# No-ops between row scatters, spins in narrower pieces, and a reordered start in a sorted-attention and expert-layer kernel

## The chip, the core and the metric

The kernel runs on one core of one Trainium2 chip. A core has a matrix engine (TensorE, PE in the profile), a vector engine (VectorE, DVE), a scalar engine (ScalarE, ACT), a general engine (GpSimd, POOL), an engine that mostly starts transfers (SyncE, SP) and 16 DMA engines. Each engine works through its own list of instructions in order and waits on semaphores for the others. The metric is the device time of one execution in microseconds; lower is better.

## What is computed

Two layers follow each other. The first is an attention whose key and value blocks are mixed by a matrix `P`, made from `sort_net` in five rounds of normalising; the second sends each of 3072 rows to one of 8 experts.

```python
# attention: batch 4, heads 8, sequence 768 in 8 blocks of 96, head size 64
for _ in range(5):
    P = exp(P - max(P, -1));  P = P / sum(P, -1);  P = P / sum(P, -2)
k_sorted = einsum('bhij,bhjcd->bhicd', P, k_b)        # the same for v
scores = q_b @ k_sb.T / sqrt(64)                      # within a block
x = softmax(scores) @ v_sb                            # -> 3072 rows of 512

# expert layer
logits = x @ w_gate + modality_bias[modality_id]
e_idx = argmax(logits);  gate_w = softmax(logits)[e_idx]
out[row] = gate_w * (relu(x @ w1[e_idx]) @ w2[e_idx]) # w1: 512x1024, w2: 1024x512
```

## The kernel before

The kernel is one straight program. Its parts, in the order of time:

1. Loads of q, k, v and of two experts' weights, issued by GpSimd; the five rounds on `P` on VectorE and ScalarE. Meanwhile TensorE multiplies ones ("spins"):

```python
wsrc = bass.AP(tensor=ones_bf.tensor, ..., ap=[ones_bf.ap[0], [0, 4], [1, 128]])   # 512 columns
def spin(n, after=None):
    for z in range(n):
        ins = nc.tensor.matmul(warm[:, z % 2], ones_bf, wsrc, start=True, stop=True)
        ...
spin(13)
for u in range(2):
    tq_pe(u)                       # transposes of q
spin(5)
...                                # in round 4: spin(4, e_ins)
```

2. The sort of k and v for the first half of the batch (`g0`: 10 jobs for k, then those for v), as matmuls into PSUM and copies out of it (L353 in the profile, matmuls L366 for k and L375 for v). `copy_out` lets a small balance decide between ScalarE and VectorE.

```python
for f, g, x0, kd in g0[:10]:       # k sort
    f(g, x0, kd)
scores(0); expo(0); mod_T()
load_k(1, 0); load_k(1, 1)
home_map(); spread_q(0, 1, nc.gpsimd); gate_w()
for n, (f, g, x0, kd) in enumerate(g0[10:]):   # v sort
    f(g, x0, kd)
    if n == 3:
        scores(1); expo(1)
```

3. 32 steps of attention. Step `u` does `scores(u)` (matmuls L418), `expo(u)` (ScalarE, L424) and `av(u - 1)` (matmuls L437, then VectorE L444 and L445). From step 16 on a step also runs one piece of the expert layer. Further work is hung onto steps: `at1` before `av`, `at2` after it. Four groups `m` of 8 steps each end in `gate_T`, `gate_L` (logits of the 768 rows of the group, four times 128 columns `c`), `choose(m)` (the best expert, on VectorE), `place(m)` and `table(m)`.

```python
for u in range(2, 32):
    p1, p2 = pace(u)               # (0, 0) before 16, then (1, 0)
    scores(u); expo(u)
    run_pieces(p1)
    for f, a in A1.get(u, []): f(*a)
    av(u - 1); prep_q(u + 2); prep_s(u + 3)
    run_pieces(p2)
    for f, a in A2.get(u, []): f(*a)
```

4. `place(m)` ranks the rows of a group within their experts (matmuls L502 to L509, VectorE L512 to L520) and sends them to a scratch buffer in DRAM, 96 rows to a scatter:

```python
def one(t):
    if t:
        if m:
            nc.gpsimd.memset(kT[0][:, 0:896], 0.0)   # L531; kT[0] is not read any more
        nc.gpsimd.nop()
    ins = nc.gpsimd.indirect_dma_start(out=xs_dram, ..., in_=xt.bitcast(I32)[:, t], ...)  # L533
for t in range(8):
    one(t)
```

`table(m)` (VectorE, L580 to L605, each on a few numbers) turns the counts into the start rows of the next expert pieces ("slots" of 256 rows); SyncE reads them and fetches the rows, transposed (L656). Slots 0 and 1 depend on group 0, slots 2 and 3 on group 1, 4 to 7 on group 2, 8 to 12 on group 3.

5. The expert layer: for each slot four pieces `mL1` (matmuls L689, relu on ScalarE L683 or VectorE L681) and two pieces `mL2` (matmuls L712, scaling L699 or L701, a scatter into the output L703). After `table(3)` every engine reads the number of rows left over and branches (L993); with this input there is none.

Of the kernel before, what the change touches and what calls it, by code (L numbers as in the profile page):

```python
# [17 lines left out]
def kernel(  # L18
# [13 lines left out]
    nc = tc.nc  # L32
# [41 lines left out]
    kT = [singles.tile([128, GC], BF16, tag=f"kT{g}", name=f"kT{g}") for g in range(2)]  # L74
# [6 lines left out]
    xTg = [singles.tile([128, 8, BLK], BF16, tag=f"xTg{z}", name=f"xTg{z}") for z in range(2)]  # L81
# [9 lines left out]
    def q_in(g, hh):  # L91
# [11 lines left out]
                                            ap=[[2 * BLK, NTL], [1, 2 * BLK]]))  # L103
# [44 lines left out]
    ones_bf = singles.tile([128, 128], BF16)  # L148
# [93 lines left out]
        eng(qT, tq.pop(u).rearrange("p t (i r) -> p i t r", r=16))  # L242

    warm = opsum.tile([128, 2, 512], FP32, tag="op", name="warm")
    wsrc = bass.AP(tensor=ones_bf.tensor, offset=ones_bf.offset, ap=[ones_bf.ap[0], [0, 4], [1, 128]])

    def spin(n, after=None):
        for z in range(n):
            ins = nc.tensor.matmul(warm[:, z % 2], ones_bf, wsrc, start=True, stop=True)
            if after is not None and z == 0:  # L250
                tc.add_manual_dep(ins.ins, after.ins.name, SYNC, reason="in step with the iterations")

    spin(13)
    for u in range(2):
        tq_pe(u)
    spin(5)
    for it in range(5):
        if it == 0:
            nc.vector.tensor_reduce(red, P_t, AX.X, ALU.max)
            nc.vector.tensor_tensor(P_t, P_t, red.broadcast_to([BH, NB, NB]), ALU.subtract)  # L260
        e_ins = nc.scalar.activation(P_t, P_t, ACT.Exp)
        if it == 4:
            spin(4, e_ins)
        if it == 3:
            tq_out(0, nc.scalar.copy)
        if it == 4:
            tq_out(1, nc.scalar.copy)
        for f in gap[it]:
            f()
        nc.vector.tensor_reduce(red, P_t, AX.X, ALU.add)  # L270
        nc.vector.reciprocal(red, red)
        nc.vector.tensor_tensor(P_t, P_t, red.broadcast_to([BH, NB, NB]), ALU.mult)
        nc.vector.tensor_reduce(red, P_swap, AX.X, ALU.add)
        nc.vector.reciprocal(red, red)
        colb = bass.AP(tensor=red.tensor, offset=red.offset,
                       ap=[red.ap[0], [0, NB], red.ap[1]])
        nc.vector.tensor_tensor(P_bf if it == 4 else P_t, P_t, colb, ALU.mult)
# [38 lines left out]
    def mod_T():  # L316
        tp = mipsum.tile([128, 64], BF16, tag="mi", name="modT")
        nc.tensor.transpose(tp[0:BLK, 0:NTL], modB.rearrange("b t r -> b (t r)"), ident[0:NTL, 0:NTL])
        nc.scalar.copy(modF, tp[0:BLK, 0:NTL])
# [20 lines left out]
    def use(act=0.0, dve=0.0):  # L340
        busy[0] += act
        busy[1] += dve
# [9 lines left out]
    def copy_out(dst, src, act, dve):  # L352
        (nc.scalar.copy if pick(act, dve) else nc.vector.tensor_copy)(dst, src)  # L353
# [54 lines left out]
    def scores(u):  # L408
        g, hf, h = unit(u)
        sc = scpsum.tile([128, 2, 512], FP32, tag="sc", name=f"sc{u}")  # L410
        qT = qTb[g][:, h * 768:(h + 1) * 768].rearrange("p (i f) -> p i f", i=NB)
        for j in range(4):
            i = hf * 4 + j
            x0 = (h * 8 + i) * BLK
            m = 128 if h * 8 + i < 63 else BLK
            for par in range(2):
                rows = slice(par * 64, (par + 1) * 64)
                nc.tensor.matmul(sc[0:m, par, j * BLK:(j + 1) * BLK],  # L418
                                 kT[g][rows, x0:x0 + m], qT[rows, i],
                                 start=True, stop=True)  # L420
        sc_tiles[u] = sc

    def expo(u):
        mark[0] = nc.scalar.activation(attnT[u % 2][:, 0:8 * BLK].rearrange("p (r f) -> p r f", r=2),  # L424
                             sc_tiles.pop(u)[0:BLK, :, 0:4 * BLK], ACT.Exp, scale=scale)
        use(act=0.82)
# [24 lines left out]
    def gate_T(m, c):  # L451
        tp = mipsum.tile([128, 8, BLK], BF16, tag="mi", name=f"gt{m}_{c}")
        for t in range(8):
            nc.tensor.transpose(tp[:, t], xb[m % 2][:, t, c * 128:(c + 1) * 128], ident[:BLK, :BLK])  # L454
        copy_out(xTg[c % 2], tp, 0.8, 0.56)

    def gate_L(m, c):
        lg = mipsum.tile([BLK, 8, E], FP32, tag="mi", name=f"lg{m}_{c}")
# [36 lines left out]
    def place(m):  # L495
        oh, ls = oh_t[m]
        xt = xb[m % 2]
        prev = ohs[m % 2]
        rk = mipsum.tile([128, 8, E], FP32, tag="mi", name=f"rk{m}")
        rkf = rk.rearrange("p t e -> p (t e)")  # L500
        pb = bass.AP(tensor=prev.tensor, offset=prev.offset, ap=[prev.ap[0], [0, 8], prev.ap[1]])
        nc.tensor.matmul(rkf, maskUT[0:BLK, :], oh.rearrange("p t e -> p (t e)"), start=True, stop=False,  # L502
                         skip_group_check=True)
        nc.tensor.matmul(rkf, ones_bf[0:BLK, :], ebase.rearrange("p t e -> p (t e)"), start=False, stop=False,
                         skip_group_check=True)
        nc.tensor.matmul(rk, ones_bf[0:BLK, :], pb, start=False, stop=False, skip_group_check=True)
        for t in range(7):
            ob = bass.AP(tensor=oh.tensor, offset=oh[:, t].offset, ap=[oh.ap[0], [0, 7 - t], [1, E]])
            nc.tensor.matmul(rk[:, t + 1:8], ones_bf[0:BLK, :], ob, start=False, stop=(t == 6),  # L509
                             skip_group_check=True)  # L510
        sel_r = small.tile([BLK, 8, E], FP32, tag="selr", name=f"selr{m}")
        nc.vector.tensor_tensor(sel_r, rk[0:BLK], oh, ALU.mult)  # L512
        dest = small.tile([BLK, 8], I32, tag="dest", name=f"dest{m}")
        dstf = small.tile([BLK, 8], FP32, tag="dstf", name=f"dstf{m}")
        nc.vector.tensor_reduce(dstf, sel_r, AX.X, ALU.add)
        nc.vector.tensor_copy(dest, dstf)
        sm = small.tile([BLK, 8, 1], FP32, tag="sm", name=f"sm{m}")
        nc.vector.tensor_reduce(sm, ls, AX.X, ALU.add)
        gcol = xt.bitcast(FP32)[:, :, Dm // 2 + 1:Dm // 2 + 2]
        nc.vector.reciprocal(gcol, sm)  # L520
        g, hf = m // 2, m % 2
        icol = xt.bitcast(I32)[:, :, Dm // 2]
        idm = idI.rearrange("p (b f j) -> p b f j", b=4, f=2)[:, 2 * g:2 * g + 2, hf]
        nc.gpsimd.tensor_copy(icol.rearrange("p (r j) -> p r j", r=2), idm)
        scat[m] = []
        use(dve=1.5)

        def one(t):
            if t:
                if m:  # L530
                    nc.gpsimd.memset(kT[0][:, 0:896], 0.0)  # L531
                nc.gpsimd.nop()
            ins = nc.gpsimd.indirect_dma_start(  # L533
                out=xs_dram, out_offset=bass.IndirectOffsetOnAxis(ap=dest[:, t:t + 1], axis=0),
                in_=xt.bitcast(I32)[:, t], in_offset=None)
            after = []
            tc.declare_no_dep(ins.ins, group="xs", reason="rows are disjoint", **({"keep": after} if after else {}))
            tc.add_to_no_dep_group("xs", ins.ins)
            for pre in after:
                tc.add_manual_dep(ins.ins, pre.name, SYNC, reason="rows leave at an even pace")  # L540
            scat[m].append(ins.ins)
        ones_[m] = one
        for t in range(8):
            one(t)
        nxt = ohs[(m + 1) % 2]
        ohsum = small.tile([BLK, E], FP32, tag="ohsum", name=f"ohsum{m}")
        nc.vector.tensor_reduce(ohsum, oh.rearrange("p t e -> p e t"), AX.X, ALU.add)
        nc.vector.tensor_tensor(nxt, ohsum, prev, ALU.add)
# [222 lines left out]
    g0 = jobs(0, kinds)  # L771
    for f, g, x0, kd in g0[:10]:
        f(g, x0, kd)
    scores(0)
    expo(0)
    mod_T()
    load_k(1, 0)
    load_k(1, 1)
    home_map()
# [2 lines left out]
    use(dve=-busy[1], act=-busy[0])  # L782
    for n, (f, g, x0, kd) in enumerate(g0[10:]):
        f(g, x0, kd)
        if n == 3:
            scores(1)
            expo(1)
    load_v(1)
# [37 lines left out]
    def at1(u, f, *a):  # L826
        A1.setdefault(u, []).append((f, a))

    def at2(u, f, *a):
        A2.setdefault(u, []).append((f, a))  # L830
# [8 lines left out]
    for m in range(4):  # L839
        for c in range(4):  # L840
            u = 8 * m + 2 * c + 3
# [10 lines left out]
    at2(8, *jb[1])  # L852
    at2(8, gate_T, 0, 3)
    at2(8, *jb[2])
    at2(8, gate_L, 0, 3)
    at2(8, choose, 0)
    at2(8, *jb[3])
    at1(9, place, 0)
    at2(3, make_bd, 1)
    at2(4, late_consts)  # L860
    j_at = [9] * 4 + [10] * 4 + [11] * 4 + [12] * 3 + [13] * 3 + [14] * 3 + [15] * 3
    for u, j in zip(j_at, jb[4:]):
        at2(u, *j)
    at2(17, place, 1)
    at1(26, place, 2)
    for m in range(3):
        at2(8 * m + 11, table_x, m)
# [161 lines left out]
```

## Time and profile before

| | |
|---|---|
| Timed, median of 3 | 200.13 us (199.83 to 202.01) |
| Profiled execution | 213.3 us |
| Mean granted TensorE clock in the profile | 0.899 |
| Row scatters L533 | 32, 931 ns each |
| Memsets L531 | 21, 862 ns each, 18.1 us in all |
| Expert matmuls L689 / L712 | 384 at 281 ns / 181 recorded at 391 and 382 ns |
| Spin matmuls L249 | 22 of 512 columns, 8.7 us |
| DMA queue of the loads and scatters | 23.10 MB, 48.5% of 16 engines' span |

The profile is one execution, and it is longer than the timed ones; it is read for the place and the cause of a wait. A busy time of PE is that of pipelined matmuls; PEld is the weight load, which goes beside them. `[2.34 <-issue]` behind an instruction says that its engine was idle for 2.34 us before it and what ended that; "issue" is time in which it waited for nothing that the profile shows. In a table of stretches each engine has its busy time and, in brackets, its instructions.

### The profile page before, as it was taken

Reading aid. Unit: us, or ns where it says so; the run is one execution under the profiler, and the core shown is the slowest. Engines: PE = TensorE matmul, PEld = TensorE weight load, DVE = VectorE, ACT = ScalarE, POOL = GpSimd, SP = SyncE. Lnnn points to the kernel's source line nnn. Section 1 sums busy time; section 2 is a strip of 40 time slices with the busy share of each in tenths; the row PEclk is TensorE's granted clock in tenths of the full one; section 3 lists DMA queues with packets and bytes.
Section 4 is the critical chain, followed back from the end, with each engine's and each line's share of the span. In section 5 each row is a group of like instructions: output and inputs, shape, how many; then the busy total and the mean of one; then the engine's idle time right before and its main releaser. Section 6 shows DMA issues by size and latency. Waiting matters only on the chain. (4 is left out here: it accounts for less than half of the span.)

```text
span 213.3 us, 5194 instructions
## 1 busy us (share of the span) xinstructions
PE 170.9 (80%) x2050; PEld 122.5 (57%) x2061; DVE 108.0 (51%) x331; ACT 93.7 (44%) x150; POOL 102.0 (48%) x139
## 2 busy tenths in 40 slices
PE   6476698777449987969599599999699999999910
PEld 2235597566329976738466475676566676765400
DVE  5977577746118787787277532557124222322200
ACT  2037468757108874946447332453213242223300
POOL 7901579901740040799408983279870623223230
PEclk9979799997855899999879658999999999999995
DMA  5999999999980559812532215853162993121210
GB/s 60 210 222 202 202 218 223 201 215 213 208 214 9 99 80 195 159 42 59 161 58 86 58 38 153 166 121 122 49 182 92 187 225 110 52 98 49 98 49 0
DMA packets 30160, 27.66 MB, mean 130 GB/s; under 512 B 18831, under 2 KB 25775, under 8 KB 29872
## 3 DMA queue, kind: packets, MB, share of 16 engines
q0 software_dynamic: 11792, 23.10, 48.5%
q1 hardware_dynamic: 18336, 4.16, 11.8%
q8 instruction: 17, 0.28, 0.5%
q14 instruction: 15, 0.12, 0.2%
HBM read 27.35 MB, written 10.52 MB: 178 GB/s over the span
## 5 line engine op out<-in xcount | busy, mean ns | idle before, releaser
L689 PE MATMUL hp<-xT,w 128*128 128x256 bf16 x384 | 49.0, 281 | 2.1 <-PEq L993 2.1
L703 POOL DMA_INDIRECT out_dram<-kvb,idg x25 | 24.6, 983 | 44.9 <-DVE kvb L701 21.2
L533 POOL DMA_INDIRECT xs_scratch<-xb,dest x32 | 29.8, 931 | 31.1 <-issue 29.1
L689 PEld LDWEIGHTS <-w 128*128 128x128 bf16 x384 | 37.2, 100 | 11.0 <-issue 2.3
L424 ACT ACTIVATE attnT<-sc 96x768 bf16<-96x768 f32 x32 | 26.0, 811 | 10.3 <-PE sc L418 10.1
L712 PE MATMUL yp<-w,hT 128*128 128x512 bf16 x90 | 23.0, 391 | 0.5 <-issue 0.2
L445 DVE TENSOR_TENSOR xb<-op,rs 96x512 bf16<-96x512 f32 x32 | 22.0, 687 | 1.3
L712 PE MATMUL yp<-w,qT 128*128 128x512 bf16 x91 | 22.3, 382 | 0.3 <-issue 0.2
L699 ACT ACTIVATE kvb<-yp,idg 128x512 f32<-128x512 f32 x15 | 10.3, 687 | 20.3 <-PE yp L712 19.0
L531 POOL MEMSET kT<- 128x896 bf16 x21 | 18.1, 862 | 0.0
L454 PE MATMUL gt<-ident,xb 96*128 96x96 bf16 x128 | 9.8, 225 | 10.1 <-DVE xb L445 9.7
L683 ACT ACTIVATE hT<-hp 128x512 bf16<-128x512 f32 x17 | 10.1, 595 | 15.1 <-PE hp L689 10.4
L681 DVE TENSOR_SCALAR qT<-hp 128x512 bf16<-128x512 f32 x10 | 6.9, 692 | 17.8 <-PE hp L689 17.8
L366 PE MATMUL ka<-bd,kvb 128*64 128x64 bf16 x384 | 10.4, 206 | 6.9 <-issue 5.6
L437 PE MATMUL op<-v_sb,attnT 96*128 96x65 bf16 x256 | 14.9, 206 | 1.3 <-DVE xb L445 0.9
L353 ACT CAST kT<-ka 128x512 bf16<-128x512 f32 (+1 forms) x16 | 9.3, 651 | 13.5 <-PE sc L418 8.1
L418 PE MATMUL sc<-qT,kT 64*128 64x96 bf16 (+1 forms) x256 | 12.9, 221 | 2.8 <-issue 1.8
L712 PEld LDWEIGHTS <-hT 128*128 128x128 bf16 x96 | 9.4, 101 | 9.9 <-issue 1.4
L701 DVE TENSOR_SCALAR kvb<-yp,idg 128x512 f32<-128x512 f32 x9 | 6.8, 751 | 16.3 <-PE yp L712 12.5
L683 ACT ACTIVATE qT<-hp 128x512 bf16<-128x512 f32 x14 | 8.2, 595 | 15.0 <-PE hp L689 11.1
L454 PEld LDWEIGHTS <-xb 96*128 96x128 bf16 x128 | 7.1, 107 | 13.4 <-DVE xb L445 12.1
L712 PEld LDWEIGHTS <-qT 128*128 128x128 bf16 x96 | 9.2, 99 | 9.6 <-issue 0.5
(182 smaller groups left out, 267.9 us busy)
## 6 DMA issues: line engine op xcount, KB each, us to landing
w<-in_moe_w_dram POOLq DMA_DIRECT2D x4, 1024.0 KB
kvb<-in_k_dram POOLq DMA_DIRECT2D x4, 768.0 KB
kvb<-in_v_dram POOLq DMA_DIRECT2D x2, 1536.0 KB
q_in<-in_q_dram POOLq DMA_DIRECT2D x4, 384.0 KB
xs_scratch<-zpad SPq DMA_DIRECT2D x3, 258.0 KB
v_sb<-in_q_dram POOLq DMA_DIRECT2D x4, 192.0 KB
v_sb<-in_q_dram POOLq DMA_DIRECT2D x2, 384.0 KB
xs_scratch<-xb,dest POOLq DMA_INDIRECT x32
```

Of the source, the lines that this page charges most:

```text
L366: nc.tensor.matmul(acc[par * 64:(par + 1) * 64, z], k_raw[:, (c0 + z) * D:(c0 + z + 1) * D], bd[g][:, par * 64:(par + 1) * 64], start=True ...
L418: nc.tensor.matmul(sc[0:m, par, j * BLK:(j + 1) * BLK], kT[g][rows, x0:x0 + m], qT[rows, i], start=True, stop=True)
L424: mark[0] = nc.scalar.activation(attnT[u % 2][:, 0:8 * BLK].rearrange("p (r f) -> p r f", r=2), sc_tiles.pop(u)[0:BLK, :, 0:4 * BLK], ACT. ...
L437: nc.tensor.matmul(ov[:, par, j], attnT[u % 2][:, c0:c0 + 128], v_sb[g][0:BLK, par * 64 + h * 8 + i, 0:D + 1], start=True, stop=True)
L445: nc.vector.tensor_tensor(xt[:, :, h * D:(h + 1) * D].rearrange("p (r j) d -> p r j d", r=2), ov[0:BLK, :, :, 0:D], rs.broadcast_to([BLK, ...
L454: nc.tensor.transpose(tp[:, t], xb[m % 2][:, t, c * 128:(c + 1) * 128], ident[:BLK, :BLK])
L531: nc.gpsimd.memset(kT[0][:, 0:896], 0.0)
L533: ins = nc.gpsimd.indirect_dma_start(out=xs_dram, out_offset=bass.IndirectOffsetOnAxis(ap=dest[:, t:t + 1], axis=0), in_=xt.bitcast(I32)[: ...
L683: mark[0] = nc.scalar.activation(dst, src, ACT.Relu)
L689: nc.tensor.matmul(hp[:, f], w_at(s, c * F + (2 * j + f) * 128, 128), xT_b[s % NX][:, c], start=(c == 0), stop=(c == 3))
L703: ins = nc.gpsimd.indirect_dma_start(out=out, out_offset=bass.IndirectOffsetOnAxis(ap=idg[:, t, 0:1], axis=0), in_=y, in_offset=None, boun ...
L712: nc.tensor.matmul(yp, hT_b[s % 2][:, fc, t * 128:(t + 1) * 128], w_at(s, 4 * F + fc * Dm, Dm), start=(fc == 0), stop=(fc == 7))
```

## The change

It has four parts.

- Between the later row scatters (groups 1 to 3) the memset of a strip that nobody reads is replaced by 11 no-ops of GpSimd. Both keep scatters apart; a no-op uses no memory.
- The spins multiply 128 columns at a time instead of 512, four times as often.
- At the start, two v-sort jobs stand ahead of the first scores, so that TensorE has work while the last copies of sorted k are made; the second scores move three jobs back.
- The chain from the last gate of group 0 to its ranking is rearranged: the last transposed copy of a group always goes to VectorE, and three more jobs of the second sort stand between its steps. `place(1)` moves from the end of step 17 to the first half of step 18.

```diff
-    wsrc = bass.AP(tensor=ones_bf.tensor, offset=ones_bf.offset, ap=[ones_bf.ap[0], [0, 4], [1, 128]])
-            ins = nc.tensor.matmul(warm[:, z % 2], ones_bf, wsrc, start=True, stop=True)
+            ins = nc.tensor.matmul(warm[:, z % 2, 0:128], ones_bf, ones_bf, start=True, stop=True)
-    spin(13)
+    spin(52)
...
-    spin(5)
+    spin(20)
...
-            spin(4, e_ins)
+            spin(16, e_ins)
... gate_T
-        copy_out(xTg[c % 2], tp, 0.8, 0.56)
+        if c == 3:
+            nc.vector.tensor_copy(xTg[c % 2], tp)
+            use(dve=0.56)
+        else:
+            copy_out(xTg[c % 2], tp, 0.8, 0.56)
... place
                 if m:
-                    nc.gpsimd.memset(kT[0][:, 0:896], 0.0)
+                    for _ in range(11):
+                        nc.gpsimd.nop(nofuse=True)
                 nc.gpsimd.nop()
... the start
-    scores(0)
-    expo(0)
-    mod_T()
     load_k(1, 0)
...
     for n, (f, g, x0, kd) in enumerate(g0[10:]):
         f(g, x0, kd)
-        if n == 3:
+        if n == 1:
+            scores(0)
+            expo(0)
+            mod_T()
+        if n == 6:
             scores(1)
             expo(1)
... steps 8 and 9
     at2(8, *jb[2])
+    at2(8, *jb[3])
     at2(8, gate_L, 0, 3)
     at2(8, choose, 0)
-    at2(8, *jb[3])
+    at2(8, *jb[4])
+    at1(9, lambda f, *a: f(*a), *jb[5])
+    at1(9, lambda f, *a: f(*a), *jb[6])
     at1(9, place, 0)
...
-    j_at = [9] * 4 + [10] * 4 + [11] * 4 + [12] * 3 + [13] * 3 + [14] * 3 + [15] * 3
-    for u, j in zip(j_at, jb[4:]):
+    j_at = [9] * 1 + [10] * 4 + [11] * 4 + [12] * 3 + [13] * 3 + [14] * 3 + [15] * 3
+    for u, j in zip(j_at, jb[7:]):
         at2(u, *j)
-    at2(17, place, 1)
+    at1(18, place, 1)
```

## The prediction, made before the changed kernel was run

> **What bounds the kernel now.** I read the page's busy shares first, then the stretches of 3 us, then the timeline around each stretch in which TensorE (PE) had little to do, and last the chain that ended last. The profiled execution took 213.3 us and the timed ones 200.13, so I use the profile for where time is lost and scale the total afterwards.
>
> ```profile
> PE 170.9 (80%) x2050; PEld 122.5 (57%) x2061; DVE 108.0 (51%) x331; ACT 93.7 (44%) x150; POOL 102.0 (48%) x139
> ```
>
> PE is busy 80% of the span, no other engine much over half. From 151.87 us on the chain of waits is a row of PE pieces (L689, L712) without holes, so the end is simply the end of PE's work: a hole or a cold stretch of PE before that point is paid in full, and one that is removed is gained, unless a transfer then comes last.
>
> The stretches show the holes (columns: stretch, length, PE, PEld, DVE, ACT and POOL busy with counts, granted PE clock, DMA share, GB/s):
>
> ```profile
> 93.00:96.00 3.00, 0.87 (x17) 0.55 (x16) 2.22 (x7) 0.78 (x2) 2.83 (x4) 1.00 0.11 33
> 102.00:105.00 3.00, 0.67 (x18) 0.47 (x16) 1.11 (x3) 0.20 (x1) 1.82 (x2) 1.00 0.49 140
> 117.00:120.00 3.00, 0.52 (x7) 0.52 (x8) 2.26 (x9) 0.67 (x2) 2.83 (x4) 0.87 0.12 33
> 120.00:123.00 3.00, 3.00 (x31) 2.32 (x30) 0.89 (x2) 1.61 (x2) 2.66 (x4) 0.50 0.26 71
> 123.00:126.00 3.00, 3.00 (x33) 2.36 (x31) 1.11 (x3) 1.40 (x2) 2.83 (x4) 0.50 0.12 34
> 126.00:129.00 3.00, 2.78 (x22) 1.81 (x22) 1.36 (x3) 0.60 (x1) 2.32 (x3) 0.50 0.23 66
> ```
>
> In two of the holes POOL is 94% busy and DVE long busy with few instructions; after the one at 117 the clock is at half for 9 us. The timeline says what DVE did (start, length, instruction, idle before and releaser):
>
> ```profile
> 115.33 1.36 DVE L581 TENSOR_SCALAR tb_ti<-tb_ti 1x8 int32<-1x8 int32 x1
> 115.81 0.86 POOL L531 MEMSET kT<- 128x896 bf16 x1
> 116.84 0.92 POOL L533 DMA_INDIRECT xs_scratch<-xb,dest  x1 [0.17 <-issue]
> 117.47 1.17 DVE L587 TENSOR_SCALAR tabR<-tb_r 1x4 int32<-1x4 f32 x1
> 117.75 0.86 POOL L531 MEMSET kT<- 128x896 bf16 x1
> 119.48 0.61 PEld L454 LDWEIGHTS <-xb 96*128 96x128 bf16 x8 [2.80 <-DVE xb L445]
> ```
>
> An operation on eight numbers takes 1.36 us and ends at 116.69; the memset ends at 116.67. The next ends at 118.64, the memset at 118.61. The same operation undisturbed takes 0.16 us. Both began while the scatter before the memset ran, so the scatter holds them up too, and the memset follows it with no gap. PE waits for the DVE work queued behind.
>
> The third place, and two smaller ones:
>
> ```profile
> 151.87 3.65 PE L689 MATMUL hp<-xT,w 128*128 128x256 bf16 x32 [2.09 <-PEq L993]
> 83.56 0.20 PE L502 MATMUL rk<-oh,maskUT 96*128 96x64 bf16 x1 [1.25 <-DVE oh L486]
> 22.20 0.25 PE L366 MATMUL ka<-bd,kvb 128*64 128x64 bf16 x4 [2.34 <-issue]
> ```
>
> The first is the branch on the count of left-over rows, which DVE computes at the end of table 3, among memsets. The second is ranking 1, asked for before its DVE chain is done. The third is PE without an instruction in the middle of a tile.
>
> **What the Trainium skill says.** (1) "Advanced Engine Details and Errata", section VectorE Performance Modes: the second Vector SBUF port is shared with GpSimd, and GpSimd instructions and two-port Vector instructions block each other. The trace agrees: the stretched DVE operations go from SBUF to SBUF, while L681, which reads PSUM, keeps its 0.69 us beside a memset at 97.84. (2) The same page, Sequencer and Instruction Queues: the sequencer queues engine instructions and executes control instructions itself meanwhile. The trace shows no no-ops, so it does not say whether they run beside a scatter. (3) "TensorE: Matmul & The Clock Gate", Part 1: after an idle window of about 3.4 us the clock falls to half. Here idle times of 2.3 and 2.5 us (at 102.2 and 117.0) were each followed by a drop, one of 2.1 us (at 93.3) was not, so it also depends on where the window lies. (4) "Runtime: NRT & Kernel Launch", Instruction fetch mechanics: instructions come in blocks of 256 (16 KiB). The instruction queue shows one packet of 16 KB at 20.01 us, inside the hole of 2.34 us.
>
> **The change, part by part.**
>
> *No-ops for memsets.* 21 memsets of 0.86 us go, seven each in placings 1 to 3, and 11 no-ops take each one's place. Small sequencer steps on SyncE (semaphore waits at 68.61, 68.68, 68.75, 68.82) follow each other at 70 ns, so I estimate 11 x 0.07 = 0.77 us. If they come after the scatter, the period is 0.92 + 0.30 (as in placing 0, which has no memset and a period of 1.22) + 0.77 = 1.99 us, against 1.95 now; if they run beside it, 1.22. So rows leave at about the same pace, or 7 x 0.73 = 5.1 us sooner per placing. What matters is DVE. A held operation can then start when the scatter ends instead of 0.86 us later.
> - Table 1: three held-up groups (L127, a pair of copies, 2.01 instead of 0.61 us; L582, 1.47; L587, 1.33), 3 x 0.86 = 2.6 us, more than the PE hole of 2.13. I leave 0.5 for scatters that still hold DVE: gain 1.6.
> - Table 2: L581 and L587, 2 x 0.86 = 1.7 of a hole of 2.52: gain 1.6.
> - Table 3: L582 (1.57) and L587 (1.32), 1.7 of a hole of 2.09: gain 1.5.
> - The clock after table 2: 9 us at 0.50 with PE 8.8 us busy, so 4.4 us lost. With a hole of 0.9 us I give even chances that it does not drop: 2.2.
> Sum 6.9.
>
> *Ranking 1 later by a piece.* Placing 1 moves behind the scores and one expert piece of step 18 (0.34 + 1.05 us). That fills most of the 1.25: gain 0.8. Its scatters start a little later; slot 2, which reads them, asks for its rows at 103.17 and first uses them at 113.97, so that is free.
>
> *Spins in pieces of 128.* 22 matmuls of 512 columns become 88 of 128: the same columns. At half clock 512 columns took 0.43 us, and six of 128 columns (L236, at 10.36) 0.82 us from the first start to the last end, about 0.11 each behind the first, four of which make 0.43. No time of its own, but 2 x 66 = 132 more PE instructions in front of everything, so that all block borders shift by half a block. That can shorten the hole at 19.86 or move it.
>
> *v sort ahead of the first scores.* At 22.45 PE is idle 0.84 us until the last copy of kT. Two v-sort tiles now go in there: up to 0.9.
>
> *First ranking.* gate_T(0,3) is copied on DVE (0.56) instead of ACT (0.80, behind two kT copies), and more sort jobs stand between its steps. PE holes of 0.39, 0.51 and 0.99 us from 45.75 to 49.7 are what can be filled.
>
> These last three lie before 63 us, where the DMA share stays near or above 1 (1.13, 1.27, 1.25 at 48, 51 and 57). The first expert rows travel behind the first expert's weights, and one scatter waited 1.78 us for them until 62.31. So front gains mostly end in a longer wait for rows: I count 0.3 of some 3.
>
> Total: 6.9 + 0.8 + 0.3 = 8.0 us in the profiled execution. The timed runs are 13 us shorter, so some of these holes must be smaller there, and a shorter hole can be taken over by the next wait. I take about 0.64 of it: 5.1 us, so **195.0 us**.
>
> **Rivals.**
> 1. *The scatter is what holds DVE.* All held operations began during a scatter. If no-ops run beside scatters, 0.92 of each 1.22 us is taken and DVE has only the gaps of 0.3 us. Then about a third of the 4.7 us of the three tables and little of the clock comes: 197 to 199. Against it: each held operation ended with the memset, not the scatter.
> 2. *Slow no-ops.* At 0.2 us each, the period is 3.4 us and the last rows leave 7 x 1.5 = 10 us later. Slot 8 has its rows asked for at 155.99 and used at 167.51, a reserve of about 8 us after some 4 of travel; PE that is 5 us ahead would wait: 202 to 205. Nothing on SyncE looks that slow.
> 3. *Fetching takes it back.* The shifted borders put a hole as at 19.86 into a place that counts, or the 231 no-ops make POOL wait for instructions during scatters: 1 to 3 us, 196 to 198.
> 4. *The cold stretch always goes* and the fetch hole too: 190 to 192.
>
> **Range and chances.** Case 4 sets the low end, 190.5; rivals 1 and 3 together nearly nothing gained, 200.0. The line for over 2% is 196.1, a little above my number; rivals 1 and 3 lie in the band, only rival 2 lies above it. Faster by over 2% 0.60, within 2% 0.33, slower 0.07.
>
> **What would show it.** Right: L581, L582 and L587 of every table below about 0.6 us; PE holes at tables 1 to 3 under 1 us; no half clock after table 2; scatters 1.2 or 2.0 us apart. The front steps: kT's last copy followed by v-sort matmuls, ranking 0 without a wait of 1 us, but the first L689 of slot 0 waiting for rows. Wrong: DVE operations that still end with a scatter after a microsecond; a scatter period over 2.5 us; or PE holes that return in the same sum at other lines, L454 or L689 behind a transfer above all.

## The result and the profile after

The changed kernel takes **192.98 us** (median of 4, 192.78 to 194.41), the kernel before 201.07 in the same comparison (199.83 to 203.62): a ratio of **0.9633** with a 95% interval of 0.9542 to 0.9724. The profiled execution took 191.1 us with a mean granted clock of 0.946. That of before was 22.2 us longer, much more than the timed difference of 8.1, so again the profiles say where and the times say how much.

The line of the page on TensorE (PE) and the others, after:

```profile
PE 160.8 (84%) x2127; PEld 122.1 (64%) x2127; DVE 100.6 (53%) x332; ACT 93.4 (49%) x149; POOL 83.3 (44%) x118
```

POOL has 21 instructions and 18.7 us less, of which the 21 memsets make 18.1. There is nothing in their place: the lists of GpSimd's instructions in the two built programs differ by these memsets alone, no no-op is in either or in the records of the traces (what took them out is not shown), and the scatters of groups 1 to 3 now follow each other 1.21 us apart, as those of group 0 always did.

Stretches of 3 us of the changed kernel, at the places that answer to those shown of before (table 1 at 79 to 82, table 2 at 100 to 103, table 3 at 121 to 124; columns as in the prediction):

```profile
79.00:82.00 3.00, 3.00 (x41) 1.93 (x38) 2.79 (x16) 2.19 (x3) 2.39 (x3) 1.00 1.13 169
100.00:103.00 3.00, 2.77 (x42) 2.22 (x41) 2.68 (x13) 2.58 (x5) 2.39 (x3) 1.00 0.36 98
121.00:124.00 3.00, 3.00 (x24) 2.15 (x22) 2.06 (x16) 1.79 (x3) 2.39 (x3) 1.00 0.99 228
```

PE is filled at tables 1 and 3, all but filled at table 2 (2.77 of 3 us), and the clock is full. Behind table 3 the branch still empties PE, as shown below. The timeline at table 1 shows what became of the held operations:

```profile
80.12 0.91 POOL L537 DMA_INDIRECT xs_scratch<-xb,dest  x1 [0.30 <-issue]
80.62 0.16 DVE L585 TENSOR_SCALAR tb_ti<-tb_ti 1x8 int32<-1x8 int32 x1
80.81 0.18 DVE L586 CAST tb_f<-tb_ti 1x8 f32<-1x8 int32 x1
81.34 0.91 POOL L537 DMA_INDIRECT xs_scratch<-xb,dest  x1 [0.30 <-issue]
81.58 0.16 DVE L591 TENSOR_SCALAR tabR<-tb_r 1x2 int32<-1x2 f32 x1
```

L585, L586 and L591 are the former L581, L582 and L587. All three begin inside a scatter's record and take 0.16 to 0.18 us; before they took up to 1.57. And the branch, with the last step of the count that it reads and the record of the branch itself on PE's sequencer (PEq or PEldq; here count, shortest, middle and longest duration in ns, first and last start):

```profile
123.30 0.14 DVE L609 CAST nrem<-tb_t 1x1 int32<-1x1 f32 x1
126.21 1.91 PE L693 MATMUL hp<-xT,w 128*128 128x256 bf16 x16
130.02 1.14 PE L693 MATMUL hp<-xT,w 128*128 128x256 bf16 x9 [1.90 <-PEq L1001]
L1001 PEldq COMPARE_BRANCH  x1: 3457/3457/3457, 126.4 to 126.4; - x1
```

The count is ready at 123.44 us. PE's sequencer reads it only at 125.80 (L944, 0.50 us) and is then 3.46 us in the branch, while the matmuls that it had handed on end at 128.1. So PE loses 1.90 us there all the same.

### The profile page after: what moved, and what is told of

It is laid out like the page before. It is cut to its first block, busy times and chain, and to the rows that moved or that the text cites. A ratio compares the mean times of both kernels' runs of the same rounds, so it can differ in the third digit from the quotient of the medians.

```text
span 191.1 us, 5316 instructions
## 1 busy us (share of the span) xinstructions
PE 160.8 (84%) x2127; PEld 122.1 (64%) x2127; DVE 100.6 (53%) x332; ACT 93.4 (49%) x149; POOL 83.3 (44%) x118
## 4 chain that ended last, share of the span: by engine, by line
PE 31%; issue 21%; DMA 18%; DVE 14%; POOL 10%; POOLq 1%; DVEq 0%
DMA kvb<-in_v_dram 9%; DMA xs_scratch<-xb,dest 9%; POOL out_dram L707 7%; PE yp L716 6%; DVE xb L444 5%; PE va L374 5%; PE hp L693 5%; PE gt L453 4%; PE op L436 4%; PE sc L417 3%; PE lg L463 2%; DVE v_sb L352 1%; DVE rs L443 1%; POOL xs_scratch L537 1%; PE tq L236 1%
## 5 line engine op out<-in xcount | busy, mean ns | idle before, releaser
L693 PE MATMUL hp<-xT,w 128*128 128x256 bf16 x384 | 46.8, 273 | 2.0 <-PEq L1001 1.9
L693 PEld LDWEIGHTS <-w 128*128 128x128 bf16 x384 | 36.3, 98 | 10.1 <-issue 2.4
L705 DVE TENSOR_SCALAR kvb<-yp,idg 128x512 f32<-128x512 f32 x9 | 6.8, 751 | 18.7 <-PE yp L716 18.7
L687 ACT ACTIVATE hT<-hp 128x512 bf16<-128x512 f32 x18 | 10.7, 596 | 11.1 <-PE hp L693 10.8
L436 PE MATMUL op<-v_sb,attnT 96*128 96x65 bf16 x256 | 13.6, 196 | 3.0 <-DVE xb L444 2.4
L374 PE MATMUL va<-bd,kvb 128*128 128x128 bf16 x128 | 13.6, 271 | 1.6 <-DMA kvb<-in_v_dram 1.6
L374 PEld LDWEIGHTS <-kvb 128*128 128x128 bf16 x128 | 12.6, 194 | 1.9 <-DMA kvb<-in_v_dram 1.7
L352 ACT CAST kT<-ka 128x512 bf16<-128x512 f32 (+1 forms) x17 | 9.9, 640 | 7.0 <-PE ka L365 7.0
L436 PEld LDWEIGHTS <-attnT 96*128 96x128 bf16 x256 | 10.7, 100 | 3.9 <-DVE xb L444 2.9
L352 ACT CAST v_sb<-va 96x512 bf16<-96x512 f32 (+1 forms) x19 | 10.9, 611 | 4.6 <-PE va L374 3.9
L242 ACT COPY qT<-tq 128x768 bf16<-128x768 bf16 x14 | 11.1, 793 | 4.0 <-PE tq L236 2.8
```

Source lines behind the costliest of these rows:

```text
L374: nc.tensor.matmul(acc[:, z], v_cols[:, d0 + z], bd[g], start=True, stop=True)
L436: nc.tensor.matmul(ov[:, par, j], attnT[u % 2][:, c0:c0 + 128], v_sb[g][0:BLK, par * 64 + h * 8 + i, 0:D + 1], start=True, stop=True)
L687: mark[0] = nc.scalar.activation(dst, src, ACT.Relu)
L693: nc.tensor.matmul(hp[:, f], w_at(s, c * F + (2 * j + f) * 128, 128), xT_b[s % NX][:, c], start=(c == 0), stop=(c == 3))
```

## The experiments

They ran in three sets, each on one chip with its own runs of the kernel before: 201.92 us on the first (198.08 to 206.97), 202.80 on the second (200.81 to 205.14) and 220.15 on the third (215.97 to 222.62). Times are medians; a ratio compares only executions within 1.5% of the fastest of their kernel with such executions of the kernel before in the same set, so it differs a little from the quotient of the medians, and b_nops, with a single such execution, has none. The theory: a memset that stands in GpSimd's queue holds back one-source operations of VectorE (DVE) between buffers in SBUF, PE waits behind them, and nothing else in the change counts. Rivals: the scatters hold DVE as well; rows that leave sooner are what helps; the front parts have a share.

**b_nops**: the kernel before with the first part of the change alone.

```diff
-                    nc.gpsimd.memset(kT[0][:, 0:896], 0.0)
+                    for _ in range(11):
+                        nc.gpsimd.nop(nofuse=True)
```

> The kernel before with the no-ops alone. Held-up theory (the memset behind a scatter holds two-port VectorE work, and PE pays for it at tables 1 to 3): most of the gain of 8 us comes, 194 to 196.5 us; table operations of VectorE at most 0.6 us, the half clock after table 2 gone. Pace theory (rows leave sooner): the same total, so this run does not tell these two apart. Front theory (spins, v sort and first ranking made the gain): 198.5 to 200.5.

Measured: 198.49 us (193.89 to 200.00). That misses the 194 to 196.5 us expected and lies at the edge of what the front theory expected, though the kernel before was also 0.9 us slower here than in the first comparison. Its trace: table operations take 0.13 to 0.33 us, and PE has no hole of 0.8 us or more at the tables. The direction fits; the size must come from the reverse.

**a_memsets**: the changed kernel with the memset back, and nothing else undone.

```diff
-                    for _ in range(11):
-                        nc.gpsimd.nop(nofuse=True)
+                    nc.gpsimd.memset(kT[0][:, 0:896], 0.0)
```

> The changed kernel with the memsets back in place of the no-ops. Held-up and pace theories: 198 to 200.5 us, scatters 1.95 us apart, VectorE table operations over 1 us again. Front theory: 193.5 to 195.

Measured: 200.78 us, ratio 1.0052 [0.9979, 1.0124]. With the memsets back the whole gain is gone, so on this chip the three other parts together bring nothing measurable. Its timeline at table 1:

```profile
83.62 0.91 POOL L536 DMA_INDIRECT xs_scratch<-xb,dest  x1 [0.17 <-issue]
83.95 1.46 DVE L585 CAST tb_f<-tb_ti 1x8 f32<-1x8 int32 x1
84.53 0.86 POOL L534 MEMSET kT<- 128x896 bf16 x1
86.03 1.32 DVE L590 TENSOR_SCALAR tabR<-tb_r 1x2 int32<-1x2 f32 x1
86.47 0.86 POOL L534 MEMSET kT<- 128x896 bf16 x1
88.21 0.51 PE L453 MATMUL gt<-ident,xb 96*128 96x96 bf16 x8 [2.14 <-DVE xb L444]
```

The CAST ends at 85.41 and the memset at 85.39; L590 ends at 87.35 and its memset at 87.33. Both begin while the scatter ahead still runs. In the changed kernel the same operations begin inside a scatter and take 0.16 to 0.30 us, so the scatter is not what holds them for over a microsecond: the memset already does so, by these records (which are rough on GpSimd), while it stands in the queue behind the scatter.

Whether an operation is held depends on where it falls. In the traces of before, b_spins and a_memsets the table operations that read one tensor of two to eight numbers and stay in SBUF behave in two ways. Those that begin between 0.23 us after the start of a scatter and the start of the memset behind it end 0.02 to 0.03 us after that memset. Those that begin at most 0.14 us after the start of the scatter take 0.15 to 0.18 us. Table 2 of a_memsets has one of the latter:

```profile
104.89 0.91 POOL L536 DMA_INDIRECT xs_scratch<-xb,dest  x1 [0.17 <-issue]
105.02 0.16 DVE L585 CAST tb_f<-tb_ti 1x8 f32<-1x8 int32 x1
107.53 0.51 PE L453 MATMUL gt<-ident,xb 96*128 96x96 bf16 x8 [0.67 <-DVE xb L444]
```

PE loses 0.67 us there, and no half clock follows, although the memsets are back. In front of the matmuls that wait at tables 1 and 2, PE is idle 2.13 and 2.52 us in before, 0.78 and 2.44 in b_spins, 2.14 and 0.67 in a_memsets. So the size of this loss changes from trace to trace.

**a_nops28**: 28 no-ops in place of 11.

```diff
-                    for _ in range(11):
+                    for _ in range(28):
```

> The changed kernel with 28 no-ops instead of 11. At 70 ns each, beside the scatter, the period should be 28 x 0.07 = 1.96 us, that of the memsets, with no memory used. Held-up theory: within 1% of the changed kernel, 192 to 195 us. Pace theory: as with the memsets, 197 to 200. If the period stays 1.22 us, a no-op takes under 44 ns and the run says nothing.

Measured: 196.43 us, ratio 0.9833 [0.9764, 0.9903], scatters 1.21 us apart. The built program is that of the changed kernel, so this is the changed kernel on this chip; neither 11 nor 28 of these no-ops set a pace.

**b_spins**: the kernel before with the narrow spins alone.

```diff
-            ins = nc.tensor.matmul(warm[:, z % 2], ones_bf, wsrc, start=True, stop=True)
+            ins = nc.tensor.matmul(warm[:, z % 2, 0:128], ones_bf, ones_bf, start=True, stop=True)
-    spin(13)
+    spin(52)
```

(and the other two spins four times as often)

> The kernel before with the spins of 128 columns alone. Held-up theory: within 0.7% of before, 199 to 201.5 us, as what it does before 63 us ends in a longer wait for the first expert rows. Front theory (the shifted borders of instruction blocks take away the hole in the middle of the k sort and what follows): 195 to 198.

Measured: 204.39 us, ratio 1.0074 [0.9952, 1.0197]: no effect that can be told from none.

**a_again**: the changed kernel itself, for comparison within the second set.

> The changed kernel once more, on the chip of the next three, as their yardstick. All theories: 0.955 to 0.985 of before.

Measured: 198.28 us, ratio 0.9755 [0.9680, 0.9830]. Here PE came to the first expert piece before its rows did:

```profile
69.73 1.87 PE L693 MATMUL hp<-xT,w 128*128 128x256 bf16 x8 [2.42 <-DMA xT<-xs_scratch]
```

The clock was at half from 69.3 to 83.0 us; the 1.87 us of this group are 1.03 in the first profile after, which had no such wait.

**a_mem_psum**: the changed kernel with the memsets back, but with the table's integer and result operands in PSUM, and the one pair of q copies that would be held moved to ScalarE. If holding is the cause this is as quick as the changed kernel although its rows leave late; if sooner rows are the cause it is as slow as a_memsets.

```diff
-                    for _ in range(11):
-                        nc.gpsimd.nop(nofuse=True)
+                    nc.gpsimd.memset(kT[0][:, 0:896], 0.0)
...
-        cp = mipsum.tile([128, E], FP32, tag="mi", name=f"cp{m}")
+        cpw = mipsum.tile([128, 4 * E], FP32, tag="mi", name=f"cp{m}")
+        cp = cpw[:, 0:E]
...
-        ti, f, a = t_("ti", E, I32), t_("f"), t_("a", 2)
-        r = small.tile([1, 2, 2], FP32, tag="tb_r", name=f"tb_r{m}")[:, 0:n]
+        ti, f, a = cpw[0:1, E:2 * E].bitcast(I32), t_("f"), t_("a", 2)
+        r = cpw[0:1, 2 * E:2 * E + 4].rearrange("p (a b) -> p a b", b=2)[:, 0:n]
...
-            spread_q(u // 16, (u % 8) // 2)
+            spread_q(u // 16, (u % 8) // 2, nc.scalar if u == 22 else None)
```

> The changed kernel with the memsets back, but with the table operations that they held up taken out of the two-port kind: their small operands lie in PSUM instead of SBUF, and the one pair of q copies that was held goes to ScalarE. Scatters 1.95 us apart as with the memsets. Held-up theory: table operations of VectorE under 0.5 us in spite of the memsets, and the time within 1% of the changed kernel. Pace theory (rows that leave sooner make the gain): as with the memsets, 2% or more above the changed kernel.

Measured: 198.37 us, ratio 0.9742 [0.9650, 0.9834], the same as a_again beside it, with scatters 1.95 us apart. Its timeline at table 1:

```profile
80.46 0.96 POOL L537 DMA_INDIRECT xs_scratch<-xb,dest  x1 [0.18 <-issue]
81.07 0.15 DVE L587 CAST tb_f<-cp 1x8 f32<-1x8 int32 x1
81.42 0.86 POOL L535 MEMSET kT<- 128x896 bf16 x1
81.81 0.15 DVE L592 TENSOR_SCALAR tabR<-cp 1x2 int32<-1x2 f32 x1
```

Both operations stand where those of a_memsets were held, one beside the scatter with a memset behind it and one inside a memset, and take 0.15 us; one that was left in SBUF, L598 at table 3, takes 0.76. From the first scatter of group 1 to that of group 3, with tables 1 and 2 between, 40.75 us pass in a_mem_psum, 40.72 in the first profile after and 40.74 in b_nops, against 43.45 in a_memsets and 46.82 in b_spins. So it is the hold that costs time in this stretch, 2.7 us in one trace and 6.1 in the other, where a half clock of 3.4 us follows it, and a pace of 1.95 us without a hold costs nothing there. For the whole kernel the argument spans two chips, as a_memsets was not run on this one, and in single traces other parts of the kernel also differ by 2 us and more. This is what the Trainium skill, "Advanced Engine Details and Errata", section VectorE Performance Modes, lets one expect: its two-port modes, the ones that meet GpSimd, need source and destination in SBUF.

**a_nospins**: the changed kernel with the wide spins of before (the diff of b_spins, reversed).

> The changed kernel with the spins of 512 columns. If the narrow spins are worth nothing: within 0.7% of the changed kernel. If their shift of instruction blocks helps the rest of the front: 1 to 2% above it, with the hole in the k sort at 19.9 us and over 2.3 us long.

Measured: 198.42 us, ratio 0.9781 [0.9705, 0.9857], as a_again. The hole in the k sort is 3.06 us long with them, against 1.80 in the first profile after and none over 0.8 in a_again. So the hole differs and the time does not move: it lies in the front, ahead of the rows that PE waits for in a_again.

**a_norank**: the changed kernel with the chain of the first ranking and the place of `place(1)` as before.

```diff
-        if c == 3:
-            nc.vector.tensor_copy(xTg[c % 2], tp)
-            use(dve=0.56)
-        else:
-            copy_out(xTg[c % 2], tp, 0.8, 0.56)
+        copy_out(xTg[c % 2], tp, 0.8, 0.56)
...
-    at1(18, place, 1)
+    at2(17, place, 1)
```

> The changed kernel with the first ranking's chain and the second ranking's place as before. By the prediction's terms 0.8 us for ranking 1 and next to nothing for ranking 0: 0 to 0.7% above the changed kernel, with a wait of 1 us or more before the matmuls of ranking 1 and a first row scatter that starts within 1.5 us of the changed kernel's. Pace theory: the same. If the chain of the first ranking sets when the first rows come: 1% or more above.

Measured: 199.12 us, ratio 0.9736 [0.9645, 0.9828], as a_again, though ranking 1 has its hole of 1.25 us again (at 75.4).

The third set was meant for the front: can the rows of slot 0 come sooner (a_latew2), and does the order of first scores and v sort count (a_nov)? The chip gave another question.

**a_third**: the changed kernel again.

> The changed kernel, yardstick for the next three on this chip. 0.955 to 0.985 of before, with PE waiting up to 2.4 us for the first expert rows at 67 us in most executions.

Measured: 235.57 us, ratio **1.0801** [1.0687, 1.0916]. The same program that gained 2 to 4% elsewhere loses 8% here.

**a_latew2**: the second half of the first expert's weights is loaded behind the first scatters.

```diff
-    load_w(0, parts=(1,))
...
     at1(9, place, 0)
+    at1(9, lambda: load_w(0, parts=(1,)))
```

> The changed kernel with the second half of the first expert's weights loaded behind the first eight row scatters instead of ahead of them. If the rows of the first slots wait behind those weights: no wait of the last scatter for the weights, first row fetch by 64 us, PE without a hole over 0.5 us before slot 0 and no half clock between 68 and 83 us, 1 to 2% below the changed kernel. If the rows come no earlier, or the weights are then late: the same or slower, with the hole in front of the first scaled output instead.

Measured: 236.89 us, ratio 1.0910 [1.0779, 1.1031]. The last scatter of group 0 waits no more, and the time does not fall.

**a_nov**: the first scores ahead of the v sort, as before.

```diff
+    scores(0)
+    expo(0)
+    mod_T()
     load_k(1, 0)
...
-        if n == 1:
-            scores(0)
-            expo(0)
-            mod_T()
-        if n == 6:
+        if n == 3:
```

> The changed kernel with the first scores ahead of the v sort as before. If what is gained in front of 63 us ends in a longer wait for the first rows: within 0.7% of the changed kernel. If the first scores' wait for kT counts (0.8 us of PE and the half clock behind it): about 0.5 to 1.5% above.

Measured: 236.54 us, ratio 1.0872 [1.0751, 1.0993]: no effect beside a_third.

**b_bare_latew2**: the kernel before without memsets and with nothing in their place, and with the late weights.

```diff
-                    nc.gpsimd.memset(kT[0][:, 0:896], 0.0)
+                    pass
```

(and the diff of a_latew2)

> The kernel before with two edits alone: no memsets (and nothing in their place), and the second half of the first expert's weights behind the first scatters. If these two are all that counts: level with the changed kernel with the late weights, within 1%. If the front of the change counts once the rows no longer wait: 1% or more slower than that.

Measured: 239.67 us, ratio 1.1032 [1.0939, 1.1125]. Of this the late weights explain little (the median of a_latew2 lies 0.6% above that of a_third). So on this chip it is the missing memsets that cost 8 to 10%, with or without the other parts of the change. Those parts together do bring something here: b_bare_latew2 lacks them and is 1.2% above a_latew2, and no execution of one reaches into the range of the other (238.87 to 240.60 and 235.55 to 238.68). a_nov shows that it is not the order of first scores and v sort; which of the other parts it is was not tested.

Where it goes, from the stretches of the four bursts of scatters, first in a_third:

```profile
52.80:64.10 11.30, 5.72 (x91) 4.09 (x91) 1.08 (x3) 1.76 (x3) 7.44 (x8) 0.50 1.06 206
86.80:96.60 9.80, 5.16 (x66) 3.42 (x68) 3.39 (x15) 2.14 (x4) 7.37 (x8) 0.96 0.64 139
116.60:126.30 9.70, 4.81 (x66) 3.42 (x65) 2.01 (x12) 2.78 (x4) 7.28 (x8) 0.84 0.33 100
150.30:160.10 9.80, 5.47 (x42) 3.75 (x41) 3.39 (x25) 2.02 (x4) 7.32 (x9) 1.00 0.44 128
```

In every burst PE is busy about half of the time (21.2 of 40.6 us; in the first profile after, 39.7 of 41.0). POOL alone keeps its pace. The timeline of a_third in the third burst:

```profile
118.55 0.48 PE L463 MATMUL lg<-wgp,xTg 128*96 128x8 bf16 x8
120.40 0.35 PE L417 MATMUL sc<-qT,kT 64*128 64x96 bf16 x8 [1.01 <-issue]
126.34 1.00 POOL L707 DMA_INDIRECT out_dram<-kvb,idg  x1 [0.30 <-issue]
129.56 0.22 DVE L469 TENSOR_TENSOR lacc<-lg,biasm 96x64 f32<-96x64 f32 x1 [9.38 <-remote]
130.67 0.82 PE L453 MATMUL gt<-ident,xb 96*128 96x96 bf16 x8 [6.03 <-DVE xb L444]
```

DVE stands still for 9.38 us in front of an operation whose input PE had written by about 119.0 ("remote": the profile knows no releaser). PE goes on in small groups with gaps for which the trace has no reason ("issue"), then stops. ScalarE waits 5.31 us for scores that PE had written by 120.8. All three start again at 129.6 to 130.7, a little over 2 us after GpSimd's last scatter in the row (126.34 and 1.00 us long). The same happens after the fourth burst, with a hole of 7.98 us at 157.3. In or around each such stretch the clock is at half, in 51.5 to 72.0, 95.9 to 102.7, 123.2 to 140.2 and 160.7 to 171.0 us; in the first profile after, the first of these lasts from 51.0 to 57.9 and the others are missing.

The profile of the kernel before holds the counterpart within one execution: group 0, whose scatters have no memset between them (about 1.23 us apart), and groups 1 to 3 with memsets (1.95 apart):

```profile
52.00:63.50 11.50, 6.08 (x95) 3.79 (x91) 1.96 (x4) 2.16 (x4) 7.48 (x8) 0.65 1.11 213
86.70:101.80 15.10, 12.91 (x192) 9.41 (x191) 11.68 (x27) 10.14 (x15) 13.60 (x15) 1.00 0.32 73
112.90:127.80 14.90, 12.16 (x147) 9.86 (x148) 7.58 (x23) 7.56 (x11) 13.37 (x16) 0.71 0.22 65
139.60:154.50 14.90, 12.76 (x96) 9.15 (x96) 7.25 (x27) 6.02 (x10) 13.38 (x16) 1.00 0.38 103
```

PE is busy 6.1 of 11.5 us in the first and 37.8 of 44.9 in the others, with DVE at 4 instructions in the first. So the other engines can be left without work during a run of scatters 1.22 us apart, and were not during those 1.95 apart in the same execution. Group 0 also differs in that its transfers fill the DMA engines (a share of 1.11), but in a_third PE starves at shares of 0.33 to 0.64 as well. No run separates the pace from the memset between the scatters. What is starved is not settled. The instruction queue does not show it: its 16 KB blocks took 0.88 to 1.47 us each in a_third and 0.88 to 1.25 in the first profile after. The Trainium skill, "Runtime: NRT & Kernel Launch", Instruction fetch mechanics, takes fetching to be mostly hidden; the gaps here look like slow delivery of instructions or of semaphore events, but that is argued and not shown. No run of this case has the kernel before's profile on the third chip, though its one profile is of an execution of 215.04 us, near the times there and not near its other times. Each set is one occasion, so chip and moment are not told apart. And a_mem_psum, which keeps the pace of 1.95 and frees DVE, was not run there; by these readings it is the version to try where chips differ.

## Why the prediction was right, point by point

The range (190.5 to 200.0) holds 192.98 and the change is faster by over 2%; the point, 195.0, is 2.0 us too high. The repeats of the first two sets gave 0.9833 and 0.9755, so the predicted 5.1 us lies between what the runs gave (3.4 to 7.4 us of 201).

- **No-ops for memsets.** Mechanism right: DVE freed, PE filled. a_memsets and a_mem_psum show it from both sides. The step "the scatter holds them up too" was wrong in the main: I left 0.5 us for it at table 1, and beside scatters alone such operations take at most 0.33 us. The same observation (held operations begin inside the scatter) had the other reading, a memset that holds from its queue place.
- **Cost of a no-op, 70 ns each.** It applies to nothing, as no no-op is in the program. The case "1.22 if they run beside it" gave the right period by luck: there is nothing to run. Rival 2, slow no-ops, fell with it.
- **Table 1, 1.6 us, and table 2, 1.6.** Right in kind: holes of 2.13 and 2.52 us are gone. The size is that of one trace, as b_spins (0.78 and 2.44) and a_memsets (2.14 and 0.67) show. A third hole of before, 2.33 us at 102.2, is 1.16 after (at 90.7); I had no term for it, and it is 1.16 in a_memsets and 1.02 in b_spins too, so it is not the missing memsets that halve it.
- **Table 3, 1.5 us.** Wrong. DVE was held there and is no longer, but the hole stayed (2.09, then 1.90). I took the branch's wait for a wait on the count. In the trace of before the count ended at 147.55 us and PE's matmuls at 149.8, so it was ready 2.2 us ahead of the hole, and 4.7 ahead after. The branch itself costs this: on PE's sequencer it lasts 3.52 us in before and 3.46 after, and the hole is what is left of it when the queued matmuls end. The end of L605 in the trace of before shows that the count was not late.
- **The clock after table 2, 2.2 us with even chances.** It did not drop in the first profile after (full from 57.9 to 184.2 us), so between these two profiles the whole 4.4 came. That the memsets made it is not shown: in a_memsets it stays full there too, and in b_spins it is at half for 3.4 us. In a_again it dropped elsewhere, behind a wait for rows.
- **Ranking 1, 0.8 us.** The hole goes and comes as foreseen (a_norank), the time does not show it; the interval of a_norank is wide enough to hide 0.8, so mis-sized at most.
- **Front, 0.3 of 3 us.** Right in kind. The 2.34 us hole became 1.80 and 1.62 (the second one waits for v from DRAM), the wait at ranking 0 went from 1.02 to 0.82 us with 1.37 soon after, and the wait for the first rows appeared in a_again as described.
- **The factor 0.64.** It stood for holes smaller in the timed runs, and each of two later traces with memsets does have one of the two holes under 0.8 us. But much of what made the profile of before long lies elsewhere: from the first scatter of group 0 to that of group 1 it took 34.5 us, against 25.4 after and 30.2 in b_spins, with PE starved beside scatters that the change leaves alone. With table 3 out of the sum, 1.6 + 1.6 + 4.4 = 7.6 us is near the 8.1 of the first comparison and above the 3.4 to 5.0 of the repeats; that the factor, taken for one reason, also covers a wrong term and an untypical execution is luck.
- **Rival 1 (the scatter is what holds DVE)** is refuted by the timelines after: a hold of at most 0.18 us is left. **Rival 3 (fetching)** did not show on the first two chips. On the third something like it takes 8% net, which neither the rivals nor the 7% for slower had foreseen: I asked what the memsets hold up and not what the pace they set keeps apart.

## What to carry to other kernels

In this kernel a memset as filler on GpSimd cost VectorE time when VectorE copied or converted from SBUF to SBUF. Such work can be freed by taking the filler out, or by putting one operand into PSUM. Before a filler is taken out, ask what its pace was for, and measure on more than one chip: here the same program gave 0.9633, 0.9755 and 0.9833 on three occasions and 1.0801 on another. Check that the instruction meant to take its place is in the built program.

## What the runs showed of the hardware

- A memset of GpSimd that is queued behind a scatter holds DVE from before its own record starts, from about 0.2 us after the start of the scatter: 0.16 us becomes up to 1.57. The operations that started a hold each read a single tensor (COPY, CAST, TENSOR_SCALAR); those behind them show long records because they wait in line. Not all such operations are held: L600 and L601 of before, on one number each and inside a memset, take 0.14 and 0.13 us.
- An indirect scatter of 96 rows keeps GpSimd 0.91 us, with 0.30 until the next. Beside it the table operations of DVE take 0.14 to 0.33 us (b_nops and the first profile after); the longer ones begin in its second half and end 0.02 to 0.04 us before its end.
- The branch on the loaded count takes 3.34 to 4.38 us on PE's sequencer (a_latew2, b_spins; all other traces between) and 0.05 and 0.07 us on ScalarE and DVE. It left PE idle for 1.4 to 3.2 us, and for about 2 whether the count was ready 2.2 or 4.7 us before the hole (before, after). Why it is long on PE is not shown.
- During and after rows of eight scatters 1.21 us apart PE, DVE and ScalarE stood without work for up to 6 to 9 us in a_third; PE was busy about half of each such row in all four traces of the third chip and in group 0 of before. In the traces of the first two sets and in the first profile after, PE was busy for 8.7 us or more of the first 9.7 of such a row.
